# An S4 convolution plus gated MLP: real and imaginary spectra on the same partitions, two units per array visit, half of the inverse's sums on VectorE

## The chip, the cores and the metric

The kernel runs on one core of one Trainium2 chip. Its time is the device time of one execution in microseconds; several executions are timed and the median is given. One further execution is recorded by the hardware profiler, and the views quoted below are views of that record.

The engines in it are TensorE (PE; PEld is its weight loading, which overlaps it), VectorE (DVE), ScalarE (ACT), GpSimd (POOL) and SyncE (SP), which here only issues DMAs. Matmul results land in PSUM, in eight banks; one bank holds 128 partitions x 512 f32. Everything else lies in SBUF. L12 is line 12 of the kernel before.

## The reference

With L = 2048 rows, D = 512 channels, N = 128 modes and F = 1792 hidden units, the output is `x + S4(LN(x)) + GLU(LN(x))`:

```python
xn = layernorm(x)                                    # over the 512 channels, no scale or shift
dt = exp(log_dt)[:, None]; logdA = dt * (A_re + 1j * A_im)
K  = einsum("dn,dnl,dn->dl", C, exp(logdA[:, :, None] * arange(L)), dt * B).real
y  = irfft(rfft(xn, 2 * L) * rfft(K, 2 * L))[:L]     # causal convolution along the rows, per channel
y  = y + xn * Dskip
g, u = xn @ w_gate, xn @ w_up                        # F = 1792
out  = x + y + (sigmoid(g) * u) @ w_down
```

All tensors are bf16, the transforms in the reference are f32.

## The kernel before, in words

**The plan.** The program builds a list of operations (`_Plan`). Each has an engine, what it depends on, and the slots that it takes (`acq`) and gives back (`rel`): PSUM tiles and pieces of SBUF. They are issued in the order of a list written out by hand, `ORDER`; within an engine, and within each DMA queue, that order is the order of execution. Slots are handed out in list order too, so an operation waits for whoever gave its slot back. `copy` (L276 to L286) makes an eviction, a copy from PSUM to SBUF: on ScalarE (L285), or on VectorE (L283) where the operation's number stands in the tuple `ON_DVE`. `UEV` names the groups of the MLP whose up product is evicted by ScalarE before the product.

**PSUM before.** Two pairs of banks (pool `s`, 128x1024 f32) serve the convolution, and four single banks (pool `gu`) the MLP:

```python
pairs = [psum.tile([128, 1024], F32, name="pair%d" % i) for i in range(NS)]
banks = [psum.tile([128, 512], F32, name="bank%d" % i) for i in range(NGU)]
```

**Stages.** First some warm-up matmuls without use (L521), the layernorm (L542 to L565) and its transposes. Beside it runs the MLP in four groups of 512 rows: gate matmuls (L1013, `fg`: a bank from four 128x128 by 128x512 matmuls), sigmoid on ScalarE (L1025; two pairs of the first group are done 1024 wide, `JOINT`, L1028), up matmuls (L1037), their eviction (L1048), the product on VectorE (L1052), and after a group's 14 products the down matmuls (L1086, `fd`).

The kernel's table `kT` is made meanwhile: powers of the modes by squaring (L655 to L666; the copies to other partitions are DMAs on GpSimd's queue, L660), complex products on VectorE (`f_a`, L722 and L723; `f_b`, L727 and L728), squares on ScalarE (L775), small matmuls (`f_k` L806, `f_sel` L826) with their evictions, and the Dskip add `f_ds` (L837).

The transform's first stage (`fx2`, L683) turns rows into 64-point pieces on 32x64 pieces of the array, evicts them 1024 wide and stores them to DRAM (`z_scr`).

Then comes a loop over the two halves p of the channels (256 each) and eight units u of the frequencies, in the order of `UNITS[p]`. For one unit: a load of 256 KB from `z_scr`; the forward matmuls `fm` (L875: four of 64x64 pieces); an eviction of 128x1024, in which the real parts lie on 32 partitions and the imaginary parts on the next 32; a **swap** of neighbouring blocks of 32 partitions, which makes the second copy for the complex product (p = 0: four DMAs of 64 KB on SP's queue; p = 1: four VectorE copies, L888); a load of `E` (320 KB) and ten matmuls `fk` (L897) for the unit's kernel spectrum, evicted 1024 wide; the products on VectorE, `fpa` (L902, 128x2048) and `fpb` (L906, 128x1024); the inverse matmuls `fv` (L919: sixteen on 64x64 pieces, four at a time, eight 512 wide and eight 256 wide); an eviction; and a store of 256 KB to `v_scr`.

At the end `v_scr` comes back in three parts per block of rows (SP issues, L418 is the line of every DMA), `s2_mm` (L979) does the last stage on the array, and it is added to the MLP's result, either on VectorE (`fe` of `final`, L992, six adds of 128x1024) or, for the last four row tiles, by going on in the bank of the down matmuls (add at L1106). The output goes out in DMAs on SP's queue, the very last on ScalarE's.

Of the kernel before, what the change touches and what calls it, by code (L numbers as in the profile page):

```python
# [40 lines left out]
NS, NGU = 2, 4  # L41
# [4 lines left out]
UNITS = ((0, 1, 2, 3, 4, 5, 6, 7), (0, 1, 6, 3, 7, 5, 2, 4))  # L46
JOINT = (2, 3)
WARM = (6, 3, 3)
# [118 lines left out]
def _build_E(M2, by):  # L167
# [9 lines left out]
    E = E.reshape(NKT, 128, NU, 128).transpose(1, 2, 0, 3)[:, by]  # L177
    E[:, 1::2] = np.roll(E[:, 1::2], 64, axis=-1)
    return E

def _consts():
# [5 lines left out]
    def quads(m, cross=False):  # L187
        m = m.transpose(1, 0, 2)
        lo, hi = m[0:64, :, 0:64].copy(), m[64:128, :, 64:128].copy()
        if cross:  # L190
            lo[:, 1::2], hi[:, 1::2] = m[64:128, 1::2, 64:128], m[0:64, 1::2, 0:64]
        return np.concatenate([lo, hi], axis=0)
# [3 lines left out]
    for q in range(128):  # L196
        sw[q, 2 * (q // 32) + q % 2, 16 + q % 32 // 2] = 1.0
    return dict(ident=f(np.eye(128)), S1=f(np.tile(S1, (4, 1))), S2=f(np.stack([_build_S2(by), np.roll(_build_S2(by), 32, axis=1)], axis=1)), M2=f(quads(M2[by])), SW=f(sw),
                MAB=f(np.stack([quads(MA[by], True), quads(MB[by], True)], axis=2)), E=f(_build_E(M2, by).reshape(128, NU // 2, 2, NKT, 128).transpose(1, 0, 2, 3, 4)))

UEV = (0, 1, 2, 3, 4, 5, 6, 7, 9, 10, 11, 14, 15, 16, 17, 18, 19, 20, 21, 22, 23, 26, 27, 28, 29, 30, 31, 32, 33, 34, 35, 36, 37, 38, 39, 40, 41, 42, 44, 45, 50, 51, 52, 54, 55,)
ON_DVE = (104, 105, 106, 119, 129, 362, 520, 843, 851,)
ON_ACT = (2,)
ORDER = [
# [111 lines left out]
def kernel(  # L316
# [25 lines left out]
    def bank(slot, r=0):  # L342
        if slot.pool == "s":
            return pairs[slot.idx][:, 512 * r:512 * r + 512]
        return banks[slot.idx][:]

    def two(slot):
        return pairs[slot.idx][:]
# [833 lines left out]
```

## Time and profile before

| | |
|---|---|
| runs, us | 218.29, 216.15, 217.68; median 217.68 |
| profiled execution, span | 216.1 us; the page gives no time around the span, and the fastest run, 216.15, is the nearest to it |
| TensorE busy | 210.2 us, 97% |
| VectorE busy | 198.2 us, 92% |
| ScalarE busy | 172.3 us, 80% |
| GpSimd busy | 31.5 us, 15% |
| DMA | 44.46 MB, mean 206 GB/s |

Busy time is the union of an engine's instructions, so a busy engine may still work in small or narrow steps. Where the prediction speaks of a distance, it is from the start of one instruction or group to the start of the next on the same engine. A row of the timeline has the start in us, the length, the engine, the line, the operation, output and inputs by name, the tile on the array for a matmul, the shapes, and how many neighbours of one kind were put together; in brackets, the idle time before it and what ended that. A row of the groups by line has the count, the busy us and mean ns of one, and the idle time of the engine just before. A row of the windows has the stretch, its length, then for PE, PEld, DVE, ACT and POOL the busy us with the count, the clock of TensorE, the DMA share and GB/s.

### The profile page before, as it was taken

The page shows a single profiled execution, that of the slowest core. Times are in us where ns is not written, and L with a number is a line of the kernel's source. Part 1 is how long each engine was busy: PE and PEld are TensorE (multiplying, and loading weights), DVE is VectorE, ACT ScalarE, POOL GpSimd, SP SyncE. Part 2 cuts the span into 40 slices and gives each one's busy share as a digit, 9 for nine tenths or more (in the row PEclk, how much of TensorE's full clock was granted, in tenths as well). Part 3 has the DMA queues.
Part 4 walks back from the last instruction along what each step waited for, and adds up shares of the span by engine and source line. Part 5 has one row for each costly group of instructions (what it writes and reads, how often), then busy time and mean ns, then how long its engine had stood idle before and what let it go on. Part 6 is the DMA issues. An engine that isn't in the chain of part 4 may idle for free.

```text
span 216.1 us, 5430 instructions
## 1 busy us (share of the span) xinstructions
PE 210.2 (97%) x2098; PEld 104.6 (48%) x2098; DVE 198.2 (92%) x439; ACT 172.3 (80%) x279; POOL 31.5 (15%) x65
## 2 busy tenths in 40 slices
PE   7999999999999999999999999999999999999995
PEld 2554444344444454545554554554546564544353
DVE  3899999899999999999999989999999999993683
ACT  2899999999999999698899999939569989753000
POOL 3232522433321200012000022000010100000200
PEclk9999999999999999999999999999999999999999
DMA  6899789586993997396864583591875896996664
GB/s 183 327 430 342 163 185 303 99 184 153 193 246 123 222 229 221 118 251 140 217 208 134 143 262 97 134 272 73 233 173 129 262 270 169 283 295 193 205 218 146
DMA packets 44044, 44.46 MB, mean 206 GB/s; under 512 B 9449, under 2 KB 35314, under 8 KB 43890
## 3 DMA queue, kind: packets, MB, share of 16 engines
q1 hardware_dynamic: 39330, 39.06, 59.9%
q0 software_dynamic: 4384, 4.73, 13.8%
q10 hardware_dynamic: 304, 0.33, 0.6%
q8 instruction: 16, 0.26, 0.5%
q14 instruction: 10, 0.08, 0.1%
HBM read 25.22 MB, written 12.07 MB: 173 GB/s over the span
## 4 chain that ended last, share of the span: by engine, by line
PE 46%; DVE 25%; ACT 12%; DMA 11%; issue 3%; SPq 0%; POOL 0%; ACTq 0%; DVEq 0%
PE bank L1086 16%; PE bank L1037 10%; PE bank L1013 6%; ACT big L285 5%; PE pair L897 5%; DMA big<-big 5%; PE pair L919 4%; DVE big L722 4%; DVE big L723 3%; ACT hT_sb L1025 3%; DMA v_scr<-big 3%; DVE big L603 3%; DVE stats L542 3%; DMA big<-z_scr 2%; DVE big L727 2%
## 5 line engine op out<-in xcount | busy, mean ns | idle before, releaser
L285 ACT ACTIVATE big<-pair 128x1024 bf16<-128x1024 f32 (+2 forms) x74 | 71.5, 998 | 8.6 <-PE pair L919 3.5
L1037 PE MATMUL bank<-xnT,wu_sb 128*128 128x512 bf16 x224 | 54.0, 380 | 0.0
L1013 PE MATMUL bank<-xnT,wg_sb 128*128 128x512 bf16 (+1 forms) x220 | 50.9, 368 | 0.4 <-ACT hT_sb L1025 0.4
L1086 PE MATMUL bank<-wd_sb,hT_sb 128*128 128x512 bf16 (+1 forms) x238 | 50.6, 367 | 0.4 <-DVE hT_sb L1052 0.3
L1086 PEld LDWEIGHTS <-hT_sb 128*128 128x128 bf16 x238 | 22.4, 98 | 25.9 <-issue 2.1
L1013 PEld LDWEIGHTS <-wg_sb 128*128 128x128 bf16 x236 | 22.0, 98 | 25.2 <-issue 3.7
L1037 PEld LDWEIGHTS <-wu_sb 128*128 128x128 bf16 x224 | 20.8, 98 | 24.8 <-issue 2.6
L1025 ACT ACTIVATE hT_sb<-bank 128x512 bf16<-128x512 f32 x52 | 30.1, 610 | 1.2 <-PE bank L1013 1.1
L1048 ACT ACTIVATE us_sb<-bank 128x512 bf16<-128x512 f32 x45 | 27.4, 622 | 2.7 <-PE bank L1037 2.7
L722 DVE TENSOR_TENSOR big<-big 128x1024 bf16<-128x1024 bf16 (+4 forms) x40 | 26.7, 668 | 0.1
L723 DVE TENSOR_TENSOR big<-big 128x1024 bf16<-128x1024 bf16 (+4 forms) x40 | 26.6, 665 | 0.0
L902 DVE TENSOR_TENSOR big<-big 128x2048 bf16<-128x2048 bf16 x16 | 19.4, 1221 | 1.3 <-issue 0.6
L897 PE MATMUL pair<-big 128*128 128x256 bf16 x160 | 19.6, 273 | 0.0
L1052 DVE TENSOR_TENSOR hT_sb<-hT_sb,us_sb 128x512 bf16<-128x512 bf16 x45 | 18.5, 419 | 1.1 <-ACT us_sb L1048 1.0
L660 POOL DMA_DIRECT2D big<-big x24 | 13.1, 552 | 32.6 <-DVE big L666 28.5
L897 PEld LDWEIGHTS <-big 128*128 128x128 bf16 x160 | 15.5, 98 | 4.6 <-issue 0.7
L775 ACT ACTIVATE sq_sb<-big 128x256 bf16<-128x256 bf16 (+2 forms) x20 | 13.2, 666 | 5.4 <-DVE big L728 4.5
L727 DVE TENSOR_TENSOR big<-big 128x512 bf16<-128x512 bf16 (+4 forms) x40 | 16.6, 415 | 0.1
L728 DVE TENSOR_TENSOR big<-big 128x512 bf16<-128x512 bf16 (+4 forms) x40 | 16.6, 415 | 0.0
L285 ACT ACTIVATE big<-big 128x256 bf16<-128x256 bf16 x36 | 15.6, 467 | 0.9 <-PE pair L806 0.9
L888 DVE COPY big<-big 32x1024 bf16<-32x1024 bf16 x32 | 13.5, 422 | 0.5
L542 DVE BATCH_NORM_STATS2 stats<-big 128x6 f32<-128x512 bf16 x15 | 10.2, 680 | 3.7 <-DMA big<-in_A_u_dram 3.7
(100 smaller groups left out, 213.2 us busy)
## 6 DMA issues: line engine op xcount, KB each, us to landing
big<-c_E SPq DMA_DIRECT2D x16, 320.0 KB, 3.9
z_scr<-big SPq DMA_DIRECT2D x16, 256.0 KB, 3.8
big<-z_scr SPq DMA_DIRECT2D x16, 256.0 KB, 3.7
v_scr<-big SPq DMA_DIRECT2D x16, 256.0 KB, 3.7
big<-big POOLq DMA_DIRECT2D x24, 128.0 KB, 3.4
big<-in_A_u_dram SPq DMA_DIRECT2D x4, 512.0 KB, 10.5
big<-big SPq DMA_DIRECT2D x32, 64.0 KB, 3.4
big<-v_scr SPq DMA_DIRECT2D x4, 512.0 KB, 5.4
```

Source lines behind the costliest of these rows:

```text
L285: nc.scalar.activation(out=get(out), in_=get(in_), func=ACT.Identity)
L722: V.tensor_tensor(out=wide(outp), in0=wide(lo), in1=mre, op=ALU.mult)
L723: V.tensor_tensor(out=wide(tb()), in0=wide(lo), in1=mim, op=ALU.mult)
L727: V.tensor_tensor(out=outp[:, :, 0], in0=outp[:, :, 0], in1=tb()[:, :, 1], op=opr)
L897: T.matmul(two(sk)[:, o:o + DW], es()[:, g, kt, :], kT[p][:, kt, :], start=kt in (0, NKT - 1), stop=kt >= NKT - 2)
L902: V.tensor_tensor(out=pp().rearrange("p q h m -> p (q h) m"), in0=xx().rearrange("p q h m -> p (q h) m"), in1=kb()[:, 0:2 * DW].unsqueeze( ...
L1013: T.matmul(bank(sl, k % 2)[:, c0:c1], w_at(w, CUT_G, kt, k), xnT[:, grp, kt, c0:c1], start=(kt == 0), stop=(kt == KT - 1))
L1025: S.activation(out=hT_sb[:, hs.idx, k % 2, :], in_=bank(sl), func=ACT.Sigmoid)
L1037: T.matmul(bank(sl), w_at(wu_sb, CUT_U, kt, k), xnT[:, grp, kt, :], start=(kt == 0), stop=(kt == KT - 1))
L1048: S.activation(out=us_sb[:, us.idx, :], in_=bank(sl), func=ACT.Identity)
L1052: V.tensor_tensor(out=h(), in0=h(), in1=us_sb[:, us.idx, :] if on else bank(sl), op=ALU.mult)
L1086: T.matmul(bank(po)[:, 0:c[1] - c[0]], hT_sb[:, hts[k // 2].idx, k % 2, jj * 128:(jj + 1) * 128], wd_sb[:, k, c[0]:c[1]], start=first and ...
```

## The change

1. **PSUM** becomes one pool `b` of eight single banks. Every eviction of 1024 becomes two of 512 in sequence (`halves`), those of the table and the final adds too.
2. **Real and imaginary parts on the same partitions.** The forward matmuls put the real spectrum into one bank and the imaginary one into another, on the same partitions (pieces of 64 rows by 32 columns), so the swap goes, the DMAs of p = 0 and the VectorE copies of p = 1. The twelve products of a unit lie in one slot; `fpa` and `fpb` have the element counts they had. The constants `E`, `MAB`, `S1` are laid out to suit.
3. **Two units per visit.** Units are taken in pairs; `fm` issues 16 matmuls, eight at a time in two passes; the inverse `fv` issues 64 in eight passes (32 rows by 64 columns), 512 and 256 wide in turn.
4. **Sums on VectorE for p = 1.** Three adds per unit (768, 768 and 512 elements, one more of 256 for unit 0) join the products beforehand, and the inverse `fvs` needs 16 matmuls 512 wide, in two passes (one extra for unit 0).
5. **Start.** Five gate groups instead of three are cut in two column halves (`NSPLIT`), the joint sigmoids go, and there are 19 warm-up matmuls for 26.
6. **New order.** `ORDER`, `UNITS[1]`, `UEV` (46 for 45) and `ON_DVE` (12 for 9) are new. At the end, the last inverse visit is followed on TensorE by 8 up matmuls, 28 down, 4 of L979, then the rest of the last stage between two runs of down matmuls; the last two of these run half as wide. The loads of `v_scr` for p = 1 also wait for the forward matmuls of p = 1 (`z_free`).

```diff
+    def halves(dst, srcs, deps, prio, hold):
+        cps = []
+        for n, sl in enumerate(srcs):
+            cps.append(pl.copy(nc, 0.48, lambda n=n: dst(n), lambda sl=sl: bank(sl), deps + cps, prio, acq=[] if n else [hold], rel=[sl]))
+        return cps
...
-            def fm(sl=sl, u=u, zx=zx):
-                for g in range(2):
-                    for b in (0, 64):
-                        o = b ^ 64 * g
-                        T.matmul(two(sl)[o:o + 64, 2 * DW * g:2 * DW * g + 2 * DW], m2[b:b + 64, 2 * u + g, :],
-                                 zx()[b:b + 64, g:4:2, :], start=True, stop=True, tile_position=(b, o))
...
-            if p == 0:
-                sws = [dma("SP", lambda xx=xx, b=b: half_of(xx, b, 1), lambda xx=xx, b=b: half_of(xx, b ^ 1, 0), deps=[ex], prio=QP,
-                           pkt=2048, hv=0.5)(64 * KB) for b in range(4)]
-            else:
-                def f_sw(xx=xx):
-                    for b in range(4):
-                        V.tensor_copy(out=half_of(xx, b, 1), in_=half_of(xx, b ^ 1, 0))
-                sws = [pl.add("DVE", 1.5, f_sw, [ex], QP)]
+        def fm(sls=sls, u2=u2, zs2=zs2):
+            for c in range(2):
+                for pos in range(4):
+                    for x in range(2):
+                        g, b = pos // 2, 64 * (pos % 2 ^ x)
+                        T.matmul(bank(sls[2 * x + c])[32 * pos:32 * pos + 32, :], m2[b:b + 64, 2 * u2[x] + g, 32 * c:32 * c + 32],
+                                 zs2[x][1]()[b:b + 64, g:4:2, :], start=True, stop=True, tile_position=(b, 32 * pos))
...
+                def fsum(pp=pp, u=u):
+                    q = pp().rearrange("p c (j k) d -> p c j k d", k=2)
+                    V.tensor_tensor(out=q[:, 0, :, 0], in0=q[:, 0, :, 0], in1=q[:, 1, :, 1], op=ALU.subtract)
+                    V.tensor_tensor(out=q[:, 1, :, 0], in0=q[:, 1, :, 0], in1=q[:, 0, :, 1], op=ALU.add)
+                    V.tensor_tensor(out=q[:, :, 1, 0], in0=q[:, :, 1, 0], in1=q[:, :, 2, 0], op=ALU.add)
...
-            def fv(u=u, sv=sv, pp=pp, pq=pq):
-                for n in range(4):
-                    q, y = n % 2, n // 2
-                    for g in range(2):
-                        ch = slice(DW * g, DW * g + DW)
-                        for b in (0, 64):
-                            o = b ^ 64 * g
-                            T.matmul(two(sv)[o:o + 64, DW * (2 * g + y):2 * DW * (g + 1)], mab[b:b + 64, 2 * u + g, q, :],
-                                     pq()[b:b + 64, q, ch] if y else pp()[b:b + 64, q, :, ch], start=n == 0, stop=n in (1, 3),
-                                     tile_position=(b, o), skip_group_check=True)
+        def fv(u2=u2, svs=svs, ps2=ps2):
+            for n in range(8):
+                q, y = n // 2, n % 2
+                c, k = ((0, 0), (1, 1), (1, 0), (0, 1))[q]
+                for pos in range(4):
+                    for x in range(2):
+                        g, b = pos // 2, 64 * (pos % 2 ^ x)
+                        T.matmul(bank(svs[2 * x + g])[b:b + 64, DW * y:2 * DW], mab[32 * pos:32 * pos + 32, u2[x], q, :],
+                                 ps2[x][1]()[32 * pos:32 * pos + 32, c, 2 + k, :] if y else ps2[x][1]()[32 * pos:32 * pos + 32, c, k:6:4, :],
+                                 start=n == 0, stop=n >= 6, tile_position=(32 * pos, b), skip_group_check=True)
+
+        def fvs(u2=u2, svs=svs, ps2=ps2):
+            for c in range(2):
+                for pos in range(4):
+                    for x in range(2):
+                        g, b = pos // 2, 64 * (pos % 2 ^ x)
+                        o, r = bank(svs[2 * x + g])[b:b + 64, :], slice(32 * pos, 32 * pos + 32)
+                        T.matmul(o, mab[r, u2[x], 2 * c, :], ps2[x][1]()[r, c, 0:4:2, :], start=c == 0, stop=c == 1, tile_position=(32 * pos, b),
+                                 skip_group_check=True)
...
+        mv_ = pl.add("PE", 0.45 if p in SUMS else 1.28, fvs if p in SUMS else fv, prods + [l_mab, l_s1], QP, acq=svs, rel=[q[0] for q in ps2], mode="Z")
...
-                if joint:
-                    mg = pl.add("PE", 0.864, fg, xnT_ready[grp] + [l_wg[piece(k)]] + ([mg] if k % 2 else []), 80 + k * 0.001,
-                                acq=[] if k % 2 else [a])
-                elif grp == 0 and k < 3:
-                    mg = pl.add("PE", 0.44, lambda fg=fg: fg(c1=256), xnT_ready[0][0:2] + [l_wg[0]], 60 + k * 0.001, acq=[a])
+                if grp == 0 and k < NSPLIT:
+                    mg = pl.add("PE", 0.44, lambda fg=fg: fg(c1=256), xnT_ready[0][0:2] + [l_wg[piece(k)]], 60 + k * 0.001, acq=[a])
```

More of the change, by code (lines that the diff above doesn't have):

```diff
@@ L396 @@
     KQ = o
-    s1 = at(OFF["pq"], [64])
+    s1, mn = (at(OFF["pq"], [2, 64])[:, n, :] for n in range(2))
     s2 = at(OFF["tmp"], [2, 64])
@@ L522, in keep_warm @@
         return pl.add("PE", 6.2 if n > 6 else 0.2155 * n, fn, (), prio, acq=[wsl], rel=[wsl])
-    warm = [keep_warm(14, -10)]
+    warm = [keep_warm(8, -10)]
     for n in WARM:
@@ new lines, in fvs @@
+        def fvs(u2=u2, svs=svs, ps2=ps2):
+            for c in range(2):
+                for pos in range(4):
[4 more added lines that the diff above has]
+                                 skip_group_check=True)
+                        if not (c or u2[x] or pos):
+                            T.matmul(o, mn[0:32, :], ps2[x][1]()[r, 1, 1:4:2, :], start=False, stop=False, tile_position=(0, 0), skip_group_check=True)
@@ L1075 @@
             last = late and jj == 3
-            pos = [_Slot("gu") for _ in range(1 + last)]
+            pos = slots(1 + last)
             r = jj % 2
```

221 lines of the change are left out of this document (107 added, 114 removed), and 81 rows, old and new, of the table ORDER.

## The prediction, made before the changed kernel had run

> **What bounds the kernel now.** I read the head of the page first, then its slices and the chain, then TensorE's timeline.
>
> ```profile
> span 216.1 us, 5430 instructions
> PE 210.2 (97%) x2098; PEld 104.6 (48%) x2098; DVE 198.2 (92%) x439; ACT 172.3 (80%) x279; POOL 31.5 (15%) x65
> PE   7999999999999999999999999999999999999995
> DVE  3899999899999999999999989999999999993683
> PEclk9999999999999999999999999999999999999999
> PE 46%; DVE 25%; ACT 12%; DMA 11%; issue 3%; SPq 0%; POOL 0%; ACTq 0%; DVEq 0%
> ```
>
> TensorE is busy from the second slice to the last but one, at the full granted clock, and VectorE nearly as long, up to about 190 us. A busy PE need not be streaming at its peak, so the next rows are read for their distances from start to start.
>
> ```profile
> 122.62 1.03 PE L1037 MATMUL bank<-xnT,wu_sb 128*128 128x512 bf16 x4
> 123.49 1.03 PE L1013 MATMUL bank<-xnT,wg_sb 128*128 128x512 bf16 x4
> 124.44 0.41 PE L875 MATMUL pair<-big,m 64*64 64x512 bf16 x4
> 124.68 0.82 PE L919 MATMUL pair<-big 64*64 64x512 bf16 x16
> 125.44 1.04 PE L1037 MATMUL bank<-xnT,wu_sb 128*128 128x512 bf16 x4
> ```
>
> Four 512-wide matmuls take 0.87 us (122.62 to 123.49), 0.216 us each: the array streams without gaps. The same four take 0.95 where the next group uses the array in pieces, so a change of mode costs about 0.1 us. Four matmuls on the four 64x64 pieces (L875) take 0.24 us, the time of one: pieces run side by side. Sixteen of L919 (eight 512 wide, eight 256 wide, four at a time) stream for 2 x 0.216 + 2 x 0.108 = 0.65 us, and 0.76 with the change of mode. So the time follows the sum of TensorE's streams, as long as VectorE keeps its lead:
>
> ```profile
> 110.00:120.00 10.00, 10.00 (x81) 5.62 (x82) 10.00 (x22) 9.83 (x17) 0.00 (x0) 1.00 0.60 177
> 180.00:190.00 10.00, 9.83 (x104) 5.28 (x103) 9.84 (x17) 7.90 (x12) 0.00 (x0) 1.00 0.88 239
> ```
>
> Columns are TensorE, weight loads, VectorE, ScalarE, GpSimd, clock and DMA. In the stage of the units (about 100 to 190 us) TensorE and VectorE are both full. Either alone, made shorter, gives little there; the change shortens both.
>
> **The change part by part. TensorE.** The forward matmuls (fm) stream as before: 16 units x 0.24 = 3.8 us become 8 visits of two 512-wide passes, 8 x 0.45 = 3.6; minus 0.2. The inverse (fv) of the first half stays: 8 x 0.65 = 5.2 against four visits of 4 x (0.216 + 0.108) = 1.3. In the second half the sums are made beforehand, and a visit has two 512-wide passes and not eight of both widths: 5.2 us become 4 x 0.45 = 1.8, with the one extra matmul of unit 0 in it; minus 3.4. Counted over both orders there are 64 changes of mode for 71; minus 0.7. The dense groups keep their 0.216 each. Sum for TensorE: **minus 4.3 us**.
>
> **VectorE.**
>
> ```profile
> L888 DVE COPY big<-big 32x1024 bf16<-32x1024 bf16 x32 | 13.5, 422 | 0.5
> L727 DVE TENSOR_TENSOR big<-big 128x512 bf16<-128x512 bf16 x16 | 6.7, 420 | 0.0
> L727 DVE TENSOR_TENSOR big<-big 128x896 bf16<-128x896 bf16 x4 | 2.5, 623 | 0.0
> L1052 DVE TENSOR_TENSOR hT_sb<-hT_sb,us_sb 128x512 bf16<-128x512 bf16 x45 | 18.5, 419 | 1.1 <-ACT us_sb L1048 1.0
> L666 DVE TENSOR_TENSOR big<-big 128x512 f32<-128x512 f32 x11 | 7.6, 690 | 0.0
> L992 DVE TENSOR_TENSOR big<-pair,glu_sb 128x1024 bf16<-128x1024 f32 x4 | 4.7, 1219 | 2.4 <-PE pair L979 2.4
> L1106 DVE TENSOR_TENSOR big<-bank,big 128x512 bf16<-128x512 f32 x3 | 2.0, 684 | 0.4 <-DMA big<-r_scr 0.4
> ```
>
> The second half loses 32 swap copies, 13.5 us. It gains for each of 8 units two sums of 768 and one of 512 elements. No row has 768; between 512 and 896 the line gives 0.555, so a unit costs 2 x 0.555 + 0.42 = 1.53, all 12.2 us busy. Neighbours overlap by about 0.08, which makes 10.3; the copies overlap by nothing. That is minus 3.2. The strided rows (L727) cost what the contiguous ones do (L1052), so I take the same rate for the strided sums. With the same overlap of 0.08 a single-bank final add is 0.60 and a double one 1.14 apart, so twelve for six cost 12 x 0.60 - 6 x 1.14 = 0.4 more; for the halved Dskip adds and three more bank copies on VectorE I add 1, an estimate from the 0.60. Sum: minus 2 us. The products keep their element counts.
>
> **ScalarE.**
>
> ```profile
> 178.25 3.82 ACT L285 ACTIVATE big<-pair 128x1024 bf16<-128x1024 f32 x4
> 17.51 1.57 ACT L1025 ACTIVATE hT_sb<-bank 128x512 bf16<-128x512 f32 x3
> 16.45 1.09 ACT L1025 ACTIVATE hT_sb<-bank 128x512 bf16<-128x512 f32 x2
> 17.09 2.75 PE L1013 MATMUL bank<-xnT,wg_sb 128*128 128x512 bf16 x12
> ```
>
> A 1024-wide eviction follows the last by 0.93 us (3.82 less one of 1.04, by three), a 512-wide one by 0.48. Two halves cost 0.03 more than the whole: 2 us over 63, and about 1 for the split table evictions. ScalarE's 20% of idle time hides it, except before 80 us, where it is busy throughout; there the 16 first-stage evictions add 0.5 us, off TensorE's path as long as sigmoids are ahead.
>
> **Start.** The fewer warm-up matmuls and the five split gate groups cost nothing: eight banks hold eight gate groups in both kernels, and the ninth waits for the first sigmoid (16.45) at 17.09. The chain of tables ahead of that sigmoid isn't changed. Without this cover the seven warm-ups would be worth 1.5 us.
>
> **DMA and waits.** The 32 transfers of the first half's swap go, and a wait of 3.4 us in each unit's chain with them:
>
> ```profile
> big<-big SPq DMA_DIRECT2D x32, 64.0 KB, 3.4
> 127.47 0.80 PE L806 MATMUL pair<-big 128*32 128x82 bf16 x64 [0.27 <-ACT big L285]
> 154.43 0.84 PE L919 MATMUL pair<-big 64*64 64x512 bf16 x16 [0.19 <-ACT big L285]
> ```
>
> They freed SP's queue, but nobody on TensorE waits for them now, so I cost that at nothing (at best TensorE's few idle tenths). A visit now waits for two units and four free banks at once, and the gate and up groups behind it on TensorE wait too. Bounds: nothing, or one more 0.48 us eviction at each of 16 visits, 7.7 us. The nearest rows are today's waits for ScalarE, 0.2 to 0.3, already in the span; I take nothing more.
>
> A rule of the Trainium skill speaks against the new visits. "TensorEngine Tiling (Array Packing)", section "Gotcha 1: PSUM Pressure", says that different row tiles cannot access the same bank at the same time; in fm the upper and the lower row tile write one bank.
>
> ```profile
> 29.27 0.42 PE L683 MATMUL pair<-big 32*64 32x512 bf16 x8
> 29.62 3.63 PE L1037 MATMUL bank<-xnT,wu_sb 128*128 128x512 bf16 x16
> ```
>
> Eight matmuls of L683 on four row tiles, two to a bank, take 0.35 us with the change of mode, not two streams of 0.216. By this row the new visits stream side by side; the row has 32x64 pieces, though, and fm's 64x32 pieces are in no row. By that rule the trace disagrees, and the rule has its rival below.
>
> **The end.** The 4.3 us become time only if the last inverse visit isn't later and its results are back in time.
>
> ```profile
> 188.96 1.49 PE L919 MATMUL pair<-big 64*64 64x512 bf16 x32
> 189.17 0.68 DVE L906 TENSOR_TENSOR big<-big 128x1024 bf16<-128x1024 bf16 x1
> 190.38 1.04 PE L1037 MATMUL bank<-xnT,wu_sb 128*128 128x512 bf16 x4
> 190.70 1.22 DVE L283 CAST big<-pair 128x1024 bf16<-128x1024 f32 x1
> 190.95 1.35 SPq L418 DMA_DIRECT2D v_scr<-big  x2
> 192.47 4.24 SPq L418 DMA_DIRECT2D big<-v_scr  x4
> 199.50 1.05 PE L979 MATMUL pair<-big 128*64 128x512 bf16 x8
> 212.84 0.42 DVE L1106 TENSOR_TENSOR big<-bank,big 128x256 bf16<-128x256 f32 x1 [0.63 <-PE bank L1086]
> ```
>
> Now VectorE ends the last product at 189.85, the last visit ends at 190.38, the eviction at 191.92, then come store and reload, and the first final matmul runs at 199.50, which 9.1 us of other work filled. Counting instructions by these rows, the changed order puts the last sum 0.8 us earlier on VectorE and the last visit within 0.5 us of its old place. So the gain falls behind it: 8 up matmuls stand there for 24. From the last visit to the first final matmul there are 8 x 0.216 + 28 x 0.216 + 0.1 = 7.9 us. The chain took at most 9.1; four half evictions, three of them in line behind a VectorE copy, add 0.7. The stall is thus between 0 and 9.1 + 0.7 - 7.9 = 1.9; I take the middle, 0.9. At the very end VectorE has all twelve single final adds (0.60) ahead of the last five; from the last final block it needs four 0.60, three 0.60 and two 0.33, 4.9 us behind a lag of 0.6, where TensorE needs 4.6 and a last add of 0.4: plus 0.4.
>
> **Sum:** 216.1 - 4.3 + 0.9 + 0.4 = **213.1 us** of span. The profiled execution's span lies at the fastest of the three runs (216.15), and the median is 1.6 above it; the changed kernel's median by the same distance is **214.7**.
>
> **The rivals.** *Four banks at once:* evictions become TensorE's bound. For it: VectorE and TensorE are already full there, and ScalarE does more pieces in less time. Against: waits for it are tenths now. Half the upper bound gives 213.1 + 3.9 = 217.0, a median of 218.6: no change; the whole of it 222.
>
> *The reload comes later still:* the third of the changed order's first final matmuls needs a third part of the reload within 1.6 us of the first, and the four SP issues above take 4.2 us. Another 2 us: 215.1, median 216.7, no change.
>
> *Pieces don't run side by side* (the mechanism of that rule): each fm, fv and fvs pass then takes two streams: 16 x 0.216 + 5.2 + 1.7 = 10.4 us, so 223.5 of span, 225 in the median, slower. It decides once passes are more than 1.4 times as long, when 4.3 is used up. Against it stands L683.
>
> *The sums run at the single rate* (L666 beside L727: 0.69 for 0.42): slower. A unit's sums then cost 2 x 0.86 + 0.60 = 2.3 for 1.3, 8.2 us over eight units; VectorE's lead of some 1.5 covers a part, and 213.1 + 6.7 = 219.8, median 221.4. It decides from a sum of 768 above 0.75 us. Against it: strided rows are not slower.
>
> *More goes than I count:* without the swaps' waits TensorE's idle tenths and the tail stall go as well, up to 2.5: 210.6, median 212.2.
>
> **How the numbers follow.** Forecast 0.55 (its own range, medians of 213.4 to 216.3 by the end's bounds); four banks 0.16; later reload 0.11; pieces 0.05; sums 0.05; more 0.08. About 1% is what a measurement of this kernel can tell from no change: its runs span 216.15 to 218.29. Faster by over 1% is below 215.5: 0.47 of the forecast, 0.08 of the last, 0.02 of the banks, 0.57. Slower is above 219.9: 0.05 + 0.05 + 0.05 of the banks, 0.15. The rest, 0.28, is within 1%. A range of 211.8 to 219.6 leaves out the two slower mechanisms, the upper half of the banks and the edge of the last.
>
> **What would show it.** Right: two-unit inverse visits of 0.45 to 0.55 us in the second half, forward visits of the same length, sums of 768 at 0.55, no 32-partition copies, TensorE idle before the first final matmul by under 2 us. Wrong: visits of 0.9, sums of 0.9, idle times "<-ACT" before visits that add up to microseconds, or a last inverse visit after 191 us.

## The result: slower

The changed kernel takes 224.19 us (median of four; 223.0 to 225.19), the kernel before 217.11 (216.15 to 218.29): a ratio of **1.032, 95% interval 1.025 to 1.039**. A ratio in this document leaves out executions more than 1.5% above the fastest of their kernel. The profiled execution has a span of 223.2 us for 216.1; around the span lie 1.8 us of the execution's 224.96. The four executions of the changed kernel have spans from 221.2 to 223.4 us, with mean granted clocks from 0.992 down to 0.975; the profiled one is among the longer.

The page's head, slices, instruction queue and chain, of the changed kernel:

```profile
span 223.2 us, 5730 instructions
PE 208.5 (93%) x2228; PEld 104.2 (47%) x2228; DVE 196.8 (88%) x445; ACT 177.0 (79%) x355; POOL 48.1 (22%) x65
PE   7999999999999999996999999999599999994794
PEclk9999999999999999999999999999889999998599
q8 instruction: 17, 0.28, 0.5%
ACT 33%; PE 27%; DVE 18%; DMA 15%; issue 5%; SPq 1%; ACTq 0%; DVEq 0%
```

TensorE has holes now, in three places, and at two of them its clock is not full. Waits of TensorE, in the same kernel ("issue" is time in which the engine waited for nothing that the profile shows):

```profile
PE bank L1004 <- DMA big<-v_scr: 4.7, 2, 3.2
PE bank L836 <- issue: 2.4, 1, 2.4
PE bank L884 <- DMA big<-z_scr: 1.9, 1, 1.9
```

And its windows around the two stretches at half clock (the column behind POOL is the clock):

```profile
160.00:164.00 4.00, 3.90 (x28) 1.63 (x28) 1.41 (x3) 2.54 (x5) 0.00 (x0) 0.57 0.81 128
200.00:212.00 12.00, 7.31 (x35) 2.94 (x34) 3.51 (x6) 0.59 (x1) 0.00 (x0) 0.72 0.63 181
```

The ledger: TensorE's idle time rose from 216.1 - 210.2 = 5.9 to 223.2 - 208.5 = 14.7 us, plus 8.8; the waits above make 8.9 (1.87, 2.35, 3.22 and 1.47 in the timeline below). The granted clock was half of full for 3.4 us in the first stretch and 6.8 in the second. That cost (1 - 0.57) x 4 = 1.7 us in the first and about 2.1, half of the 4.2 us that TensorE worked, in the second: plus 3.8. Busy time fell by 1.7, so the work itself fell by 1.7 + 3.8 = 5.5. Together: -5.5 + 3.8 + 8.8 = 7.1, the difference of the spans. **The matmuls were saved; waits and half clock took more.** Two of the new visits in the timeline:

```profile
175.22 0.63 PE L884 MATMUL bank<-big,m 64*32 64x512 bf16 x16
181.04 0.65 PE L941 MATMUL bank<-big 32*64 32x512 bf16 x16
```

And the sums, in the groups by line (count, busy us, mean ns, idle before):

```profile
L915 DVE TENSOR_TENSOR big<-big 128x768 bf16<-128x768 bf16 x8 | 4.4, 554 | 0.1
L917 DVE TENSOR_TENSOR big<-big 128x512 bf16<-128x512 bf16 x8 | 3.4, 425 | 0.3
```

The three holes in TensorE's timeline:

```profile
105.87 0.63 PE L884 MATMUL bank<-big,m 64*32 64x512 bf16 x16 [1.87 <-DMA big<-z_scr]
156.88 0.86 PE L836 MATMUL bank<-big,sw 128*32 128x96 bf16 x63
160.10 0.20 PE L836 MATMUL bank<-big,sw 128*32 128x96 bf16 x1 [2.35 <-issue]
193.88 0.75 PE L941 MATMUL bank<-big 32*64 32x512 bf16 x16
196.47 6.21 PE L1095 MATMUL bank<-wd_sb,hT_sb 128*128 128x512 bf16 x28
205.89 1.06 PE L1004 MATMUL bank<-big 128*64 128x512 bf16 x4 [3.22 <-DMA big<-v_scr]
208.94 2.77 PE L1004 MATMUL bank<-big 128*64 128x512 bf16 x12 [1.47 <-DMA big<-v_scr]
```

The transfers behind them, from the chain that ended last (start, length):

```profile
99.47 6.35 DMA big<-z_scr
192.66 2.94 DMA v_scr<-big
196.79 4.64 DMA v_scr<-big
202.10 6.80 DMA big<-v_scr
```

The first forward visit (105.87) needs two units, and the second unit's load took 6.35 us. At 157.7 TensorE stops inside one group of 64 matmuls, for nothing that a semaphore shows. The part of `v_scr` that waits for the last store is another one now. In the kernel before, it was loads of 128 KB (the first issued at 194.84, when the store had landed); in the changed one it is four loads of 384 KB (from 201.49). The DMA view has the size and the median time to landing, of the kernel before and of the changed one:

```profile
big<-v_scr SPq DMA_DIRECT2D x2, 128.0 KB, 3.1
big<-v_scr SPq DMA_DIRECT2D x4, 384.0 KB, 7.1
```

At the end 12.0 us lie between the start of the last inverse visit (193.88) and the first final matmul, with 8 us of other work; before, they were 10.5 (188.96 to 199.50), all filled.

### The profile page after: what moved, and what is told of

Same layout as the page of the kernel before. It is cut to its first block, busy times and chain, and to the rows that moved or that the text cites. A ratio compares the mean times of both kernels' runs of the same rounds, so it can differ in the third digit from the quotient of the medians.

```text
span 223.2 us, 5730 instructions
## 1 busy us (share of the span) xinstructions
PE 208.5 (93%) x2228; PEld 104.2 (47%) x2228; DVE 196.8 (88%) x445; ACT 177.0 (79%) x355; POOL 48.1 (22%) x65
## 4 chain that ended last, share of the span: by engine, by line
ACT 33%; PE 27%; DVE 18%; DMA 15%; issue 5%; SPq 1%; ACTq 0%; DVEq 0%
ACT big L292 9%; ACT us_sb L1062 6%; DMA v_scr<-big 6%; PE bank L1051 6%; PE bank L1036 6%; PE bank L1095 6%; ACT hT_sb L1045 6%; DVE big L731 4%; DVE big L732 4%; ACT big L665 4%; PE bank L899 4%; DMA big<-v_scr 3%; DMA big<-z_scr 3%; DVE big L737 2%; PE bank L1004 2%
## 5 line engine op out<-in xcount | busy, mean ns | idle before, releaser
L292 ACT ACTIVATE big<-bank 128x512 bf16<-128x512 f32 (+2 forms) x151 | 82.1, 642 | 9.5 <-PE bank L836 3.5
L1051 PE MATMUL bank<-xnT,wu_sb 128*128 128x512 bf16 x224 | 55.0, 384 | 0.2
L1036 PE MATMUL bank<-xnT,wg_sb 128*128 128x512 bf16 (+1 forms) x244 | 54.5, 362 | 0.5 <-ACT glu_sb L292 0.3
L1045 ACT ACTIVATE hT_sb<-bank 128x512 bf16<-128x512 f32 x56 | 34.5, 648 | 1.1 <-PE bank L1095 1.0
L1036 PEld LDWEIGHTS <-wg_sb 128*128 128x128 bf16 x244 | 23.0, 98 | 24.0 <-issue 3.6
L1062 ACT ACTIVATE us_sb<-bank 128x512 bf16<-128x512 f32 x46 | 29.5, 663 | 1.0 <-DVE hT_sb L1066 1.0
L899 PE MATMUL bank<-big 128*128 128x256 bf16 x160 | 19.8, 277 | 0.0
L708 POOL TENSOR_TENSOR pre<-pre,xnT 128x4 f32<-128x4 f32 x3 | 17.7, 5905 | 0.2
L784 ACT ACTIVATE sq_sb<-big 128x256 bf16<-128x256 bf16 (+2 forms) x20 | 13.8, 689 | 3.4 <-DVE big L737 2.7
```

What stands on the lines that cost most here:

```text
L292: nc.scalar.activation(out=get(out), in_=get(in_), func=ACT.Identity)
L899: T.matmul(bank(sk[kt == NKT - 1])[:, DW * c:DW * c + DW], es()[:, c, kt, :], kT[p][:, kt, :], start=kt in (0, NKT - 1), stop=kt >= NKT - 2)
L1036: T.matmul(bank(sl)[:, c0:c1], w_at(w, CUT_G, kt, k), xnT[:, grp, kt, c0:c1], start=(kt == 0), stop=(kt == KT - 1))
L1045: S.activation(out=hT_sb[:, hs.idx, k % 2, :], in_=bank(sl), func=ACT.Sigmoid)
L1051: T.matmul(bank(sl), w_at(wu_sb, CUT_U, kt, k), xnT[:, grp, kt, :], start=(kt == 0), stop=(kt == KT - 1))
L1062: S.activation(out=us_sb[:, us.idx, :], in_=bank(sl), func=ACT.Identity)
```

## The experiments

My theory after this reading: waits at three places and the half clock behind them are the loss. The rival: an engine is the bound, so a wait taken away comes back elsewhere. Edits of the order are given as the sequence on the queue or engine. Times in brackets are spans of the profiled execution; the changed kernel's is 223.2. All runs but combo, combo2, ups_behind and ups_vs are one execution, and the changed kernel's own spans lie up to 2.2 us apart, so a smaller difference of spans says nothing by itself, and the rows of the timeline decide. A line of the changed kernel can be one or two off in an experiment's rows (L836 is L835 there).

**First visit's loads.**

```diff
 SP, 89 to 100 us
-z_scr store x4, MAB load, z_scr store, z_scr load, E load, z_scr load, E load
+z_scr store x5, z_scr load x2, E load x2, MAB load
```

> The changed kernel with two SP issues moved: the load of MAB goes behind the first two loads of E, and the second z_scr load goes directly behind the first. Theory (three waits): the 1.87 us that TensorE waits at 104.0 us for the second unit's z_scr load (issued 99.47, landed 105.83) shrink to under 0.5 us, because the last z_scr store no longer lands behind 512 KB of MAB and the load no longer behind 320 KB of E; the span falls by 1 to 2 us (to 221 to 222) and the later waits stay as they are. Rival (an engine is the bound): VectorE or the evictions set the pace, so the wait goes but the last inverse visit stays at 193.9 us within 0.5 and the span at 223.

Measured (222.0): the wait for z_scr is gone, but 0.6 us later TensorE stops inside L836:

```profile
105.57 0.34 PE L835 MATMUL bank<-big,sw 128*32 128x96 bf16 x13
107.21 0.73 PE L835 MATMUL bank<-big,sw 128*32 128x96 bf16 x51 [1.30 <-issue]
192.72 0.74 PE L940 MATMUL bank<-big 32*64 32x512 bf16 x16
204.71 1.06 PE L1003 MATMUL bank<-big 128*64 128x512 bf16 x4 [3.28 <-DMA big<-v_scr]
```

The last visit is 1.2 us earlier, the end still 12.0 us behind it. This doesn't show that the order of the loads made the wait. Five runs below leave this place as it was (z_late, apart, one_load_late, sums_on_pe, last_on_pe) and have no such wait either: there the second unit's load landed 4.3 to 4.9 us after its issue instead of 6.35, and TensorE stopped for 0.5 to 1.6 us inside L836. In last_on_pe:

```profile
104.25 0.62 PE L884 MATMUL bank<-big,m 64*32 64x512 bf16 x16
106.01 0.73 PE L836 MATMUL bank<-big,sw 128*32 128x96 bf16 x51 [0.86 <-issue]
```

Nor did z_order gain time here: the gate matmuls behind L836 start at 107.87, in the changed kernel at 107.22. Its last visit is earlier because no half clock followed its stop of 2.25 us at the later L836; in the changed kernel that half clock cost 1.7 us.

**The stop without a release.** The 2228 matmuls of the changed kernel and as many weight loads came in 17 packets of 16 KB on the instruction queue, one packet for 262 instructions.

```diff
 def fu: up matmuls of the first N groups
-    matmul(bank(sl), w, xnT[..., :])
+    for c in (0:256, 256:512): matmul(bank(sl)[:, c], w, xnT[..., c])
```

> The changed kernel with the first 24 up groups computed in two column halves: the same arithmetic, 192 more TensorE instructions ahead of 95 us, at 0.01 us each group. Theory (code): the 2.35 us stop at 157.7 us, inside the 64 matmuls of L836, is TensorE running out of instructions, whose 16 KB packet started only at 157.71, when the burst of z_scr loads had ended. With the packets' places moved by 192 of 256 instructions, the packet for this place is asked for at about 150 us, ahead of the burst, and the stop goes, with the half clock from 160.4 to 163.8 behind it: about 4 us, a span near 219.5. A shorter stop may appear at another burst of small matmuls. Rival (data): the matmul waits for something that it reads or writes; then the stop stays at the same matmul with the same 2.3 us.

> As code_192, but with 16 groups, 128 more instructions. Theory (code): here the packet is asked for at about 154.6 us, in the middle of the z_scr loads and at the start of the 128 small matmuls of L815, so instructions run out earlier than in the changed kernel, at about 157 us by its clock or just before, and TensorE stands for 2 to 3.5 us; the span stays within 1.5 us of 223.2 or is longer. Rival (data): the same stop at the same matmul, 2.3 us, as in code_192.

Measured (222.7 and 227.1): the stop of 2.35 us is gone in both, and others stand elsewhere. TensorE's timeline of code_192, and then of code_128:

```profile
131.62 0.92 PE L815 MATMUL bank<-big 128*32 128x82 bf16 x76
134.72 0.68 PE L815 MATMUL bank<-big 128*32 128x82 bf16 x52 [2.18 <-issue]
```

```profile
106.22 0.41 PE L815 MATMUL bank<-big 128*32 128x82 bf16 x23 [3.11 <-issue]
140.03 0.38 PE L815 MATMUL bank<-big 128*32 128x82 bf16 x20 [2.06 <-issue]
```

The DMA view has the packet itself: in the changed kernel none on the instruction queue from 145.8 to 157.6 us and one in the 1.2 us after that, during the stop; in code_192 one between 132.4 and 133.5, where that kernel stops. Two rows of it in the changed kernel: the busy tenths of the DMA engines in 40 slices of 145.8 to 157.6, and the instruction queue from 157.6 to 158.8 (packets, MB, share).

```profile
DMA  0000000000000000000399689999999999999999
q8 instruction: 1, 0.02, 5.1%
```

So the stop moves with the count of instructions and not with the data: **TensorE waits for its own code.** The count says it more sharply. When the changed kernel stops, 3521 matmuls and weight loads have started; in z_order, last_on_pe and every other run that still stops inside this L836 and whose trace is complete, it is 3521 as well. The stops elsewhere come after 1729, 1985, 2497, 2753 or 3265. All 27 such stops ahead of 200 us, in 15 complete traces, lie on one grid of 256 instructions (13 x 256 + 193 = 3521, 6 x 256 + 193 = 1729), whatever the matmul there reads. In each of them TensorE went on 1.3 to 1.5 us after the end of a packet, and that packet had started 0.2 to 3.7 us (2.5 in the changed kernel) after TensorE had begun the 256 instructions before the stop. Stops marked "issue" among the final matmuls don't lie on the grid.

code_192's span hardly fell, against the 219.5 expected, since a wait of 2.16 us for E took the place of the other. code_128's stop at the place that the changed kernel reaches at 157 us was only 0.7 us, not the 2 to 3.5 expected.

```diff
 kernel before: the same edit of fu, 16 groups
```

> The kernel before, with 16 up groups in two column halves, 128 more instructions on TensorE, as in code_128. Theory (the new order puts runs of small matmuls together): in the kernel before at most 299 matmuls and weight loads start in any 3 us, in the changed one up to 393, at three places. So a place of a code packet that falls into such a run costs the kernel before at most a short stop, under 1 us each and under 2 us in all, and its span stays within 2 us of 216. Rival (the place of the packets alone decides, the kernel before only lay well): stops of 2 us and more at L806 or L826, and a span of 219 or more.

Measured (221.8, 5.7 us above the kernel before), mostly the rival's way, but at L919, where it had named L806 and L826:

```profile
155.30 0.73 PE L919 MATMUL pair<-big 64*64 64x512 bf16 x12 [0.19 <-ACT big L285]
158.43 0.30 PE L919 MATMUL pair<-big 64*64 64x256 bf16 x4 [2.39 <-issue]
```

Of the 5.7 us, 2.4 are this stop and about 1.7 the half clock behind it (3.4 us from 159.3). So the kernel before can stop for code too; as it stands, its packets lie well. The changed order does put more small matmuls in a row, up to 393 starts of matmuls and weight loads in 3 us for 299, but that isn't needed for a stop.

**Loads and small matmuls around the stop.**

```diff
 SP, 151 to 165 us
-z_scr load x4, E load ...
+z_scr load, E load, z_scr load x2, E load ..., z_scr load   (z_late; apart)
+z_scr load x3, E load ..., z_scr load                       (one_load_late)
 TensorE (apart, one_load_late)
-L815 x128, 4 gate, L836 x64, L884, 4 up
+L815 x128, 4 gate, 4 up, L836 x64, L884
```

> The changed kernel with three of the four z_scr loads that SP issues between 151.5 and 154.9 us moved behind the next loads of E (two of them) and behind a later one (the third, which is needed at 184 us). Theory (code behind transfers): the 16 KB packet that started at 157.71 in the changed kernel, 2.5 us after its place in the count of instructions, starts at 155 to 156.5, and the stop of 2.35 us inside L836 shrinks to under 1.2 us, with the half clock from 160.4 gone; span 219.5 to 222. Rival (the run of small matmuls alone is too fast for any packet): the stop stays above 1.8 us at the same place, and the span at 223.

> As z_late, and an up group more between L815 and L836 there (0.96 us of TensorE in which 8 instructions are used instead of 128). Theory (code): the stop is shorter than in z_late by 0.9 us or gone; span as z_late or up to 1 us less. Rival (the matmul of L836 waits for its data, the evictions of L815): the stop moves with L836 and stays as long.

> The changed kernel with the up group of apart between L815 and L836 at 157 us, and only the one z_scr load moved that is needed last, at 184 us; the two for the visit at 168 us stay. Theory (code): the packet there starts at about 156.8 us, TensorE stops for 0.3 to 1.2 us instead of 2.35, without the half clock from 160.4 and without the wait of 2 to 3 us for z_scr loads at 165 that z_late and apart had; the last inverse visit starts 2.5 to 4 us earlier than 193.9. Rival (waits only change places): the visit stays at 193 or later.

Measured (224.1, 222.1, 219.4). TensorE's timeline in z_late, then in apart, then in one_load_late:

```profile
158.50 0.20 PE L835 MATMUL bank<-big,sw 128*32 128x96 bf16 x1 [0.74 <-issue]
167.64 0.37 PE L883 MATMUL bank<-big,m 64*32 64x512 bf16 x1 [2.82 <-DMA big<-z_scr]
```

```profile
158.91 0.24 PE L835 MATMUL bank<-big,sw 128*32 128x96 bf16 x5 [0.51 <-issue]
166.78 0.37 PE L883 MATMUL bank<-big,m 64*32 64x512 bf16 x1 [2.06 <-DMA big<-z_scr]
```

```profile
159.75 0.24 PE L835 MATMUL bank<-big,sw 128*32 128x96 bf16 x5 [0.82 <-issue]
165.50 0.62 PE L883 MATMUL bank<-big,m 64*32 64x512 bf16 x16
```

With fewer loads in the burst the packet comes earlier (156.1, 156.5 and 157.2 for 157.7 us) and the stop falls from 2.35 to between 0.5 and 0.8 us: the code had stood behind data. z_late shows it alone, since its TensorE runs as the changed kernel's up to the stop (the same L836 starts at 156.90 and 156.88): the packet is 1.6 us earlier, and so is the matmul behind the stop. Seven runs that leave loads and order as they were there stop for 2.25 to 3.55 us, the changed kernel among them. In apart and one_load_late the four up matmuls help as well. In the first two the next visit then waits for its own loads. one_load_late has no such wait and no half clock there; its last visit starts at 191.86, 2.0 us earlier, and its span is 3.8 us less.

A wider mixture:

```diff
 SP: z_order; fu: code_192; TensorE (spread)
+4 gate between L836 and L815 (99 us), L899 between L931 and L815 (131), 4 up ahead of L836 (157)
```

> The changed kernel with z_order's two moves, code_192's split up groups, and three groups of TensorE moved in between runs of small matmuls: a gate group between L836 and L815 at 99 us, L899 between L931 and L815 at 131 us, an up group before the last L836 at 157 us. Theory (code): stops of TensorE with no release shown fall from 2.3 to under 1 us in all; those left are waits for transfers (E near 166 us). The last inverse visit starts at 190 to 191.5 instead of 193.9 and the span is 218.5 to 220.5. Rival (an engine is the bound): the stops go, others take their place, and the visit stays at 193 within 1.

Measured (230.9), a miss on both sides: waits of 1.99 and 3.22 us for loads of E stood in place of the stops, one stop of 1.04 us and two of 0.2 were left, and four stretches of half clock came in all. The last visit started at 202.08, against 190 to 191.5 expected and about 193 by the rival.

**The sums.**

```diff
-if p in SUMS: fsum; fvs
+no fsum, fv for all visits (sums_on_pe), or for the last pair of units alone (last_on_pe)
```

> The changed kernel without any sums on VectorE: all inverse visits take the eight passes, in the same order. VectorE loses 12 us, TensorE gains 4 x 0.85 = 3.4 us. Theory (both are full, VectorE decides the last visit): TensorE's 3.4 us are paid in full as long as nothing waits, so the last visit starts at 193 to 196 and the span is 222 to 226. Rival (the sums on VectorE are the loss): without them the span falls below 219.

> The changed kernel, in which the last pair of units of the second half is summed on TensorE, as in the first half (eight passes instead of two), and its six sums on VectorE go. Theory (VectorE sets the last inverse visit): VectorE has 3.0 us less ahead of it, so the visit starts 2 to 3 us earlier, at 191 to 192 instead of 193.9, lasts 1.4 instead of 0.6, and the span falls by 1 to 2.5 us. Rival (TensorE sets it): TensorE had its 16 up matmuls to do until 193.8 and is full anyway; the visit starts at 193.5 or later and the span rises by 0.5 to 1 us.

Measured (224.3 and 224.4). Without sums the last visit starts at 196.38, 2.5 us later: the sums on VectorE do pay. With the last pair alone on TensorE the visit starts at 192.84, right behind the 16 up matmuls. It follows the visit before it by 5.00 us (187.84 to 192.84), as in the changed kernel (188.88 to 193.88), so 3 us less on VectorE moved nothing: TensorE's own work sets that place, as the rival said. The 1.0 us that it is earlier was gained before, where no half clock followed this run's stop of 3.55 us at L836. In the changed kernel the last sum on VectorE ends at 193.93, level with TensorE; neither engine is the cause of the loss.

**The end.**

```diff
 TensorE (tail_fill)
+12 matmuls that nobody reads, ahead of the first final matmul; 6 behind L981
 SP (tail_order)
-v_scr load 512 KB, load 128 KB, store x2, load 128 KB, reload 384 KB x3, ...
+store x2, load 128 KB, reload 384 KB, load 128 KB, reload 384 KB x2, load 512 KB, ...
```

> The changed kernel with 18 matmuls added whose result nobody reads: 12 (2.6 us) between the last of the 28 down matmuls and the first final matmul, 6 (1.3 us) between L981 and the next final matmuls, where TensorE stood still for 3.22 and 1.47 us. Theory (wait, then half clock): the waits for the reload stay, the first final matmul still starts at 206 us within 0.5, but the clock stays full, so the work from 205.9 to 211.6 runs without the 2.1 us that half a clock costs it, and the span falls by 1.5 to 3 us, to 220 to 221.7. Rival (the half clock costs nothing, the reloads set the pace there too): span 223 within 0.7, and the later final matmuls wait for the transfers instead.

> The changed kernel with two v_scr loads moved on SP's queue: the 512 KB one of the last block of rows and one of 128 KB, both issued at 193 to 194 us ahead of the last two stores, go behind the reloads that the first final matmuls wait for. Theory (transfers in the way): the last store, which took 4.6 us to land (196.79 to 201.43) where that of the kernel before took 2.9, lands at 200 or before, the first final matmul starts at 203.5 to 204.5 instead of 205.89, the stop of 3.22 us shrinks to 1 to 2 us, and the span falls by 1.5 to 4 us, the more if the half clock from 204.75 goes as well. Rival (latency alone): store and reload take as long without the other transfers; the first final matmul stays at 205.9 within 0.5 and the span at 223.

Measured. tail_fill (221.9): full clock at the end. From the first final matmul to the end of the span it took 15.3 us (206.56 to 221.9), the changed kernel 17.3, which is the 2.1 us that the half clock was to cost. tail_order (224.9): the last store landed in 2.27 us instead of 4.64, but the reload of 384 KB behind it took 4.5 us, no less than the changed kernel's 4.3. The first final matmul came 10.0 us after the last visit instead of 12.0, but the next ones waited and half clock fell on the down matmuls:

```profile
204.49 0.62 PE L1003 MATMUL bank<-big 128*64 128x512 bf16 x4 [1.06 <-issue]
207.73 1.05 PE L1003 MATMUL bank<-big 128*64 128x512 bf16 x8 [2.30 <-DMA big<-v_scr]
211.06 5.46 PE L1094 MATMUL bank<-wd_sb,hT_sb 128*128 128x512 bf16 x14
```

**Sums of repairs.**

```diff
 z_order in both; unread matmuls at the end
+apart, tail_order, 16 unread     (combo)
+one_load_late, 18 unread         (combo2)
```

> The changed kernel with z_order, apart and tail_order together, and 16 unread matmuls at the end that keep the clock (4 ahead of the first final matmul, 8 and 4 between the next ones). Theory (waits and half clocks are the loss): the wait at 104, the stop at 157 and all half clocks go, the last inverse visit starts at 189 to 191 instead of 193.9 and the span is 215 to 218, a time within 1% of the kernel before (ratio 0.99 to 1.01). Rival (an engine is the bound, or other waits take their place): the span stays above 220, ratio above 1.02.

combo (224.4, ratio 1.045, 1.035 to 1.055) held the wait for loads of z_late. The next without it:

> one_load_late with z_order and with tail_fill's 18 unread matmuls at the end. Theory (the waits named and their half clocks are the loss): 223.2 less about 1.1 (z_order), 3.5 (stop and half clock) and 1.2 (tail_fill) is a span of 217 to 218.5, and a ratio to the kernel before of 0.995 to 1.015. Rival (waits only change places): span above 220.5 and a ratio above 1.02.

combo2 (220.0, full clock throughout in its profile): ratio **1.026 (1.018 to 1.034)**. The rival is half right: the last visit came at 191.57, but from there to the first final matmul it was 12.3 us again, 2.6 of them filled with matmuls that do nothing. So work was put behind the last visit, and it was done earlier:

```diff
 TensorE, from 187 us (ups_behind; last pair summed on TensorE, z_order and one_load_late in it)
-visit, 4 gate, 16 up, last visit, 8 up, 28 down
+visit, 4 gate, 4 up, last visit, 20 up, 28 down
 SP: tail_order
```

> one_load_late with z_order, with the last pair summed on TensorE as in last_on_pe, the last inverse visit put ahead of the up groups whose time it doesn't need (20 up matmuls stand behind it instead of 8), its stores ahead of the up groups' work and tail_order's two loads behind the first reloads. Theory (the end of the changed order has too little work behind its last visit): the visit starts at 188.5 to 190 instead of 191.9, TensorE has 10.4 us of work from its end to the first final matmul, where the chain of store and reload takes 9 to 11, and waits under 1.5 us instead of 3.1; span 215.5 to 218, ratio to the kernel before 0.99 to 1.01. Rival (transfers alone set the end: four reloads of 384 KB after the stores): the waits move to the later final matmuls, the span stays at 219 or above, ratio 1.015 or more.

Three of its four executions lay 4.1 to 5.4 us above the fourth (221.04), so there is no verdict, and the profile is of the longest (224.5). In it the visit starts at 190.09, but the last store leaves only at 196.26: ScalarE's evictions waited for the stores of the visit before, which fills both of the slots (`vs`) on the way to DRAM. ScalarE's waits:

```profile
ACT big L291 <- DMA v_scr<-big: 4.0, 3, 2.3
```

```diff
-vs=2
+vs=4 in the second half (four_vs: the changed kernel; ups_vs: ups_behind)
```

> The changed kernel with four SBUF slots instead of two for the results of the inverse matmuls on their way to v_scr, once the table is done. Theory (a visit of two units fills both slots, so its second eviction waits until the store of the visit before has landed): ScalarE's waits for v_scr stores (0.24 and 0.29 us near the end) go, the last store is issued at 196.0 to 196.5 instead of 196.79, and the span falls by 0.3 to 1 us. Rival (the slots aren't felt here): no difference beyond 0.3 us in the place of the last store.

> ups_behind with the four slots. There ScalarE waited 2.26 and 1.49 us for stores of the visit before, so its earlier last visit (190.09) got its last store out only at 196.26. Theory (the slots kept the gain of the earlier visit): the last store is issued 2 to 3.5 us earlier, at 192.5 to 194, the first final matmul has its data before TensorE comes to it, the later ones wait under 1.5 us together instead of 3.5, span of the undisturbed runs 215.5 to 218, ratio to the kernel before 0.99 to 1.01. Rival (the reloads set the end): the later final matmuls still wait 3 us or more and the span stays at 219.

four_vs (221.4): no wait of ScalarE for v_scr stores is left, and the last store is issued 2.5 us after the last visit's start (195.58) instead of 2.9. ups_vs (219.8): the visit starts at 190.11, as in ups_behind, the last store is issued at 193.68 instead of 196.26, and TensorE, in its timeline, waits for no reload any more:

```profile
190.11 1.89 PE L932 MATMUL bank<-big 32*64 32x512 bf16 x64
197.07 6.21 PE L1096 MATMUL bank<-wd_sb,hT_sb 128*128 128x512 bf16 x28
203.20 0.62 PE L1005 MATMUL bank<-big 128*64 128x512 bf16 x4
204.07 1.65 PE L1005 MATMUL bank<-big 128*64 128x512 bf16 x12
```

Its ratio is **1.011 (1.000 to 1.023)**, from two of its four executions (221.14 and 218.14). The other two (221.71, which is the profiled one, and 222.22) lie close to the slower of these; the medians of all, 221.42 and 217.22, give 1.019. Among what is left are two stops at L836, 1.8 us together, and the very end, where single final adds on VectorE and the output's transfers run until 4.9 us after the last matmul of the result (before: 3.3). No version here beat the kernel before.

## Why the prediction was wrong

It said 214.7 (211.8 to 219.6), faster; it is 224.2, slower.

- **TensorE's sum was right.** Two-pass visits are mostly 0.55 to 0.60 us with the change of mode, eight-pass ones 1.44 to 1.62; the work fell by 5.5 us for 4.3 forecast. The rest may be the seven warm-up matmuls (1.5 us) that I had taken as hidden. The Trainium skill, "TensorEngine Tiling (Array Packing)", section "Gotcha 1: PSUM Pressure", would have row tiles that write one bank take turns; the visits of two streams at 0.45 plus the mode change disagree with it.
- **VectorE and the sums were right**: 554 ns for 768 elements (0.555 forecast), busy minus 1.4 for minus 2. ScalarE gained 4.7 us for 3, and no wait for it counts: *four banks at once* didn't come.
- **"I take nothing more" failed** (DMA and waits). I bounded a two-unit visit by evictions; what the first one waited for was two loads (1.87 us at 104), and where that wait was missing in other runs, a stop for code of 0.5 to 1.6 us stood behind it. In costing the transfers at nothing I left out what else uses the DMA engines: TensorE's code. No step had that term, 2.35 us and 1.7 of half clock. Moving the instruction count alone moved it, so where the packets happen to lie is part of it.
- **"The end" failed by size.** I took a chain of at most 9.1 + 0.7 us from the last visit's end and a stall of 0.9; it took 11.3 (194.6 to 205.89) and the stalls were 4.7, with 2.1 of half clock. The 9.1 was a bound from the work that covered the chain; in the kernel before, its last part had landed after 7.6 (197.96). The store took 4.64 us behind 768 KB of other loads, for 2.9 before and 2.27 in tail_order. The reload took 4.31 for 3.1, and here the other loads aren't the reason, since tail_order took 4.5: it carries 384 KB where 128 KB waited for the last store before, which the prediction doesn't count. Both `vs` slots are full after one visit besides. *The reload comes later still* was the right rival, priced at 2 us; it was 3.8 above the stall I forecast, and the half clock.
- **The last visit** "within 0.5 us of its old place" came 4.9 us later: the 5.9 us of the first two waits and their half clock, less gains.

Shown: the code stops (the grid, and z_late, which moves loads alone), the price of the half clock at the end (tail_fill), and the two slots once the last visit comes early (ups_behind against ups_vs). Only argued: that the order of loads makes the wait at 104 (z_order), what more work behind the last visit is worth by itself (ups_behind has the edits of four other runs in it), and how the 8.9 us of waits would split in the other executions. Not tried: an order that ends with the units of the 128 KB part. Open: how far ahead a code packet can be fetched, and whether the order can be laid so that none falls badly.

## What to carry to other kernels

A change that makes an engine's work shorter moves the work behind it closer: before it is priced, ask for each transfer's round trip what work is left to cover it, and whether its buffers hold what one bigger visit delivers at once. A TensorE stop of a microsecond or two with nothing released, inside a run of matmuls, can be its code arriving late: look for the instruction packet in the DMA view, and see whether such stops lie a multiple of 256 instructions apart. Compare variants at several instruction counts before one is believed, since 128 instructions more cost the kernel before 5.7 us. Before a move is credited with a gain, look whether runs without it differ as much at that place, as they did at 104 us. A wait of two microseconds on TensorE may be paid twice, by the half clock behind it.

## What the hardware showed unexpectedly

TensorE's half clock came in stretches of 3.4 or 6.8 us, most of which began between 1.1 us before and 1.1 us after the end of a stop of some 2 us or more: in the changed kernel from 160.4 to 163.8 and from 204.75 to 211.6. Not every such stop had one. The one at L836 had it in the changed kernel (2.35 us) but not in z_order (2.25) and last_on_pe (3.55), nor had code_128's of 3.11 us. With the waits at the end filled by unread matmuls and the others short it didn't come in combo2's profile (1.000), though one of its four executions was granted 0.992. The Trainium skill, "TensorE: Matmul & The Clock Gate", Part 1 (the HAM clock gate), has the clock at half or full rate alone, decided over windows of about 3.4 us that run free of the program; the traces agree. A code packet of 16 KB took 0.9 to 2.0 us on its queue, and TensorE went on 1.3 to 1.5 us after it (133.4 to 134.72 in code_192). The Trainium skill, "Runtime: NRT & Kernel Launch", section "Instruction fetch mechanics", has code fetched in blocks of 16 KiB or 256 instructions, and calls crossing into the next one mostly hidden; the size agrees, and so does the grid of 256; the hiding does not, with 2.35 us of stop in the changed kernel.
